# Attention into a Hyena gate on one core: rest values as 64-row couples, one PSUM pool, 1 KB query runs, halved first weights, and a new order

## The chip, the cores and the metric

One core of a Trainium2 chip runs the kernel. The metric is the device time of one execution in microseconds (us). The profile and the trace belong to one execution each and count from the first to the last instruction; that span is some 1.8 us shorter than the device time. Engines: PE is TensorE, PEld its weight loads, DVE VectorE, ACT ScalarE, POOL GpSimd, SP SyncE (it only issues transfers).

## The reference, cut to what matters

```python
# q, k, v: (8, 12, 448, 64) f32
scores = q @ k.transpose(0, 1, 3, 2) / 8
e = np.exp(scores - m)                                 # m: maximum of a row
attn = e / (e.sum(-1) + np.exp(-m) + 1e-9)             # softmax off by one
x = (attn @ v).transpose(0, 2, 1, 3).reshape(8, 448, 768)
x1, x2, x3 = np.split(x @ w_proj, 3, axis=-1)          # w_proj (768, 2304)
x2c = irfft(rfft(x2, axis=1) * rfft(filter_fft, axis=0), n=448, axis=1)
out = (x1 * x2c * x3) @ w_out                          # w_out (768, 768)
```

A sequence of 448 rows is three blocks of 128 and a rest of 64. The twelve heads are worked in six pairs, and a batch is attention for six pairs followed by the dense part (projection, filter, gate, output projection).

## The kernel before

The kernel carries its own scheduler. Every piece of work is a task with an engine, a cost in us, a wanted time, and what it needs, makes, takes and gives back. The scheduler plays the machine forward with these costs and so fixes the order of each engine's instructions. Engines then run that order strictly.

```python
class Plan:
    LANDING = 1.8            # us from the end of a transfer's share to "landed"
    def transfers(to):       # the scheduler's picture of the transfers
        ...                  # the two queues (SyncE, GpSimd) share the engines by cost
        done(h[2], clock + self.LANDING, "SP")
```

The first two batches are "staged": f32 is loaded by SyncE and cast by GpSimd or VectorE. Later batches are loaded with a cast by GpSimd (bf16 straight into one natural-layout buffer `nat` that holds `kn` and `qn`), then transposed by SyncE's DMA transposes into `kT` and `qT`.

```python
# staged query: two transfers a pair, 256 B runs
for u in range(2):
    nc.sync.dma_start(src[0:SP, 256*u : 256*u+256].rearrange("p (j d) -> p j d", j=NST),
                      q[b, 2*hp+u].rearrange("(j p) d -> p j d", j=NST))
# a later batch: its loads may start when the batch before has been transposed out of nat
room = ["zero kn" if b == NSTAGED else ("turn", b - 1)]
add("POOL", 0.95, want + STEP*n, lambda st=st: q_load(st), need=room, make=[("qn", b)], dma=1.6, ...)
... # 8 key loads, 1 value load
for u in range(2):           # the rest rows of v, copied by GpSimd to a block-diagonal tile
    nc.gpsimd.tensor_copy(vr[b % 2][c, :, u, 0:DH], vn[b % 2][c, :, 3, 0:DH])
```

Attention's output for the rest rows was one matmul over both heads, against that block-diagonal value tile:

```python
nc.tensor.matmul(op[:, n, :, :], e[0][:, o:o+128], vr[b % 2][:, hp, :, :], start=True, stop=False)
```

The dense part starts with x transposed (one transfer a pair of heads, the last pair by TensorE), then "folded" by VectorE in two groups of three pairs:

```python
add("SP", 1.3, w, x_dma, need=[("xb", i)] + old, make=[("X", i), ("xT", b, hp)], dma=0.5)
...
def first(ds, n):            # the fold
    if n == 0:
        nc.vector.tensor_copy(x[:, ds, S:S+2], x[:, ds, 0:2])
    nc.vector.tensor_tensor(t[...], lo, hi, op=(ALU.add, ALU.subtract)[n])
w = ready - (0.4 if g else PERIOD / 4)     # wanted time of the second and the first group
```

PSUM was three pools: two double banks for scores, one bank for attention's output, three for the rest.

The softmax here doesn't subtract the row's maximum and nothing guards it: scores larger than these inputs give would overflow.

Of the kernel before, what the change touches and what calls it, by code (L numbers as in the profile page):

```python
# [41 lines left out]
class Plan:  # L42
# [12 lines left out]
    OPEN = 9  # L55

    def __init__(self, rings):
        self.size = rings
        self.tasks = []

# [3 lines left out]
    def run(self):  # L64
# [9 lines left out]
        when = {}  # L74
        held = {r: [] for r in self.size}
        holds = set()
        gone = {}
        free = {e: 0.0 for e in queue}
# [6 lines left out]
        def done(t, end, by):  # L85
            for k in t[6]:
                made[k] -= 1
                when[k] = (max(end, when.get(k, (0.0, by))[0]), by)
                heapq.heappush(events, end + self.LAT[by])
                heapq.heappush(events, end)  # L90
            for tok in t[8]:
                left[tok] -= 1
                if left[tok] == 0:
                    gone[tok] = end + self.LAT[by]
                    heapq.heappush(events, gone[tok])

# [18 lines left out]

        def ready(t):
# [9 lines left out]
            if e == "SP" and t[9]:  # L126
                out = sum(h[2][12] for h in queues[e]) + sum(x > now + 1e-9 for x in landed)
                if out + t[12] > self.OPEN:
                    return False
            new = {}  # L130
            for r, tok in t[7]:
                if (r, tok) in holds:
                    continue
# [7 lines left out]
        while any(queue.values()):  # L141
            moved = False
            for e in queue:
# [8 lines left out]
                moved = True  # L152
                for r, tok in t[7]:
                    if (r, tok) not in holds:
                        holds.add((r, tok))
                        held[r].append(tok)
# [12 lines left out]
            if not moved:  # L169
                while events and events[0] <= now + 1e-9:  # L170
                    heapq.heappop(events)
                if any(queues.values()):
                    heapq.heappush(events, now + 0.1)
# [10 lines left out]
def kernel(  # L184
# [15 lines left out]
    SPIN = 40  # L200
    EARLY1 = 14.0
    SLOT1 = 5.5
    BASE2 = 77.0
    READY1 = 80.0
    READY0 = 34.0
    BPS = 8.2
    ZV = 8.0
    RE1 = 4.0
    FT = 8.0
    GATES = (  # L210
        (1, [("iv", 5), ("ir", 1), ("ik", 7), ("iq", 7)]), ("F", [("cv", 8)]), (0, [("cv", 9)]), (2, [("cv", 10)]),
        ("O", [("cv", 11)]),
    )
    STEP = 1.5
    FOLD0 = (28.5, 29.0, 29.5)
# [3 lines left out]
    psc = ctx.enter_context(tc.tile_pool(name="psc", bufs=2, space=bass.MemoryType.PSUM))  # L219
    pop = ctx.enter_context(tc.tile_pool(name="pop", bufs=1, space=bass.MemoryType.PSUM))  # L220
    phy = ctx.enter_context(tc.tile_pool(name="phy", bufs=3, space=bass.MemoryType.PSUM))
# [27 lines left out]
    vr = [const.tile([128, NHP, 2, DH + 1], BF16, name=f"vr{i}") for i in range(2)]  # L249
# [8 lines left out]
    KNAT, SLOT = NHP * 4 * 128, 1280  # L258
    nat = const.tile([128, max(KNAT + NST * D, 8 * SLOT)], BF16, name="nat")
# [4 lines left out]
    def stage(g, at, n):  # L264
        o = g % 4 * SLOT + at
# [5 lines left out]
            "sc": 2, "op": 1, "hy": 3, "e": 6, "er": 2, "k0": 2, "q0": 2, "u": 1, "w": 1, "xf": 1,  # L271
# [5 lines left out]
    ATT0, SLOT0 = 6.0, 3.5  # L277
    PERIOD = 43.5
    BASE = 31.0

    def tau(i, frac=0.0):

        if i < NHP:
            return ATT0 + SLOT0 * (i + frac)
        if i < 2 * NHP:
            return BASE + SLOT1 * (i + frac - NHP)
        return BASE2 + (i + frac - 2 * NHP) * PERIOD / NHP

# [11 lines left out]
    def staged(b):  # L300
# [3 lines left out]
        for hp in range(NHP):  # L304
# [5 lines left out]
            for n, (name, x, at, size) in enumerate(parts):  # L310
                src = stage(g, at, size)

                def load(name=name, x=x, src=src, hp=hp, g=g):
                    if name == "q":
                        for u in range(2):
                            (nc.sync if g else nc.scalar).dma_start(
                                src[0:SP, 256 * u : 256 * u + 256].rearrange("p (j d) -> p j d", j=NST),
                                q[b, 2 * hp + u].rearrange("(j p) d -> p j d", j=NST),
                            )
# [8 lines left out]
                add("ACT" if first else "SP", 1.04 if name == "q" else 0.52, -21.0 if first else want + 0.1 * n, load, need=need,  # L328
                    make=[("s" + name, g)], dma=0.97 if name == "q" else 0.64, run=256 if name == "q" else 768,
                    n=2 if name == "q" else 1, begun=[("i" + name, g)])  # L330
                if hp == 0 and name != "q":
                    add("SP", 0.5, want + (0.05 if name == "k" else SLOT0 + 0.05) if b == 0 else want - RE1 + 0.1 * n,
                        lambda name=name, x=x: nc.sync.dma_start(rests[:, "kv".index(name)], shared(x, b)),
                        need=[("cr" + name, b - 1)] if b else (), make=[("r" + name, b)],
                        dma=0.75, begun=[("ir", b)])
# [31 lines left out]
            if hp == 0:  # L367
                for u in range(2):
# [7 lines left out]
                    add("POOL", 0.56, tau(g) + 1.0,  # L376
                        lambda c=c, u=u: nc.gpsimd.tensor_copy(vr[b % 2][c, :, u, 0:DH], rests[c, 1]),
                        need=[("rv", b), ("ones", b % 2)] + ([("V", NHP * (b - 1) - 1, 1)] if b >= 2 else []), make=[("crv", b), ("vr", b)])

            def turn(g=g, hp=hp):  # L380
                T[g]["ps"] = tps = phy.tile([128, 512], F32, name="tps", tag="hy")
                tb = tps.bitcast(BF16)
                if g:
                    nc.tensor.transpose(tb[:, 0:128], ks[:, hp, :], ident_bf)
                for t in range(1, 4):
                    nc.tensor.transpose(
                        tb[:, t * 128 : (t + 1) * 128], T[g]["kn"][:, t - 1, :], ident_bf
                    )
                for j in range(NST):
# [4 lines left out]
            def k_back(g=g, hp=hp):  # L394
                tb = T[g]["ps"].bitcast(BF16)
# [8 lines left out]
            def q_back(g=g, hp=hp):  # L404
                tb = T[g]["ps"].bitcast(BF16)
                to, of = qT[b % 2][:, hp, :], tb[:, 512 : 512 + S]
# [6 lines left out]
            def turn0():  # L413
                T[0]["ps0"] = tps = phy.tile([128, 512], F32, name="tps0", tag="hy")
                nc.tensor.transpose(tps.bitcast(BF16)[:, 0:128], ks[:, 0, :], ident_bf)

            def back0():
                nc.vector.tensor_copy(kT[0][:, 0, 0, :], T[0]["ps0"].bitcast(BF16)[:, 0:128])

            if g == 0:  # L420
# [4 lines left out]
            add("PE", 0.45, w, turn, need=[("ck", g), ("cq", g), "ident"] + ([("crk", b)] if g else []), make=[("T", g)],  # L425
                take=[hy], give=[("k0", g), ("q0", g)])
            old = [("S", g - 2 * NHP, 3)] if b >= 2 else []
            back = "ACT" if g == NHP else "DVE"
            add(back, 0.33, w + 0.1, q_back, need=[("T", g)] + old, make=[("qT", g)], give=[hy])
            add(back if g else "ACT", 0.36, w + 0.2, k_back, need=[("T", g)] + old, make=[("kT", g)], give=[hy])  # L430

    def loaded(b):
# [3 lines left out]
        want = tau(i0) - 40.0  # L436
        start = want if b > NSTAGED else 0.0
        room = ["zero kn" if b == NSTAGED else ("turn", b - 1)]

        def q_load(st):  # L440
            nc.gpsimd.dma_start(
                qn[:, st].rearrange("p (h d) -> p h d", h=H),
                q[b, :, st * SP : (st + 1) * SP, :].rearrange("h p d -> p h d"),
            )

        def k_load(u, t):
            c = slice(64 * u, 64 * u + 64)
            if t < 3:
                nc.gpsimd.dma_start(kn[:, :, 1 + t, c], kr[:, :, 4 * u + t, :])  # L449
            else:  # L450
                nc.gpsimd.dma_start(kn[c, :, 0, c], kr[c, :, 3, :])

        n = 0
        for st in range(NST):
            add("POOL", 0.95, want + STEP * n, lambda st=st: q_load(st), need=room, make=[("qn", b)], dma=1.6, after=start + STEP * n)
            n += 1
        for u in range(2):
            for t in range(4):
                add("POOL", 0.85, want + STEP * n, lambda u=u, t=t: k_load(u, t), need=room,
                    make=[("kn", b)], dma=1.0, after=start + STEP * n)  # L460
                n += 1
        add("POOL", 2.05, want + STEP * n,
            lambda: nc.gpsimd.dma_start(
                vn[b % 2][:].rearrange("p g t d -> p (g t) d")[:, :, 0:DH],
                v[b].rearrange("h s d -> (h s) d").rearrange("(n p) d -> p n d", p=128),
            ),
            need=room + [("V", i0 - NHP - 1, 1)], make=[("vn", b)], dma=6.0, after=start + STEP * n)
        for u in range(2):
            c = slice(64 * u, 64 * u + 64)
            add("POOL", 0.9, want + 22.0,  # L470
                lambda u=u, c=c: nc.gpsimd.tensor_copy(vr[b % 2][c, :, u, 0:DH], vn[b % 2][c, :, 3, 0:DH]),
                need=[("vn", b), ("V", i0 - NHP - 1, 1)], make=[("vr", b)])

        def q_turn(st):
            nc.sync.dma_start(
                qT[b % 2][:, :, st * SP : (st + 1) * SP], qn[:, st], transpose=True
            )

        def k_turn(gs):
            nc.sync.dma_start(  # L480
                kT[b % 2][:, gs].rearrange("p g t c -> p (g t) c"),
                kn[:, gs].rearrange("p g t c -> p (g t c)"),
                transpose=True,
            )

        last = ("S", i0 - NHP - 1, 3)
        for st in range(NST):
            add("SP", 1.4, want + 24.0, lambda st=st: q_turn(st), need=[("qn", b), last],
                make=[("turn", b)] + [("qT", i0 + i) for i in range(NHP)], dma=0.6)
        for h in range(NHP):  # L490
            add("SP", 0.9, want + 24.0 + h, lambda h=h: k_turn(slice(h, h + 1)), need=[("kn", b), last],
                make=[("turn", b), ("kT", i0 + h)], dma=0.6)
# [68 lines left out]
    def more_tables():  # L561
        bb = lambda: W["bps"].bitcast(BF16)[:, 0 : 4 * (FQ + 1)].rearrange("p (a b) -> p a b", a=4)

        def mirror():
            W["rps"] = rps = phy.tile([128, 512], F32, name="rps", tag="hy")
# [4 lines left out]
        def mirror_back():  # L570

            rps = W["rps"]
# [619 lines left out]
```

## Time and profile before

| | before |
|---|---|
| device time, median of 3 | 388.97 us (387.98 to 389.45) |
| profiled span | 386.9 us |
| TensorE busy | 369.1 us, 95% |
| VectorE, ScalarE busy | 69%, 68% |
| TensorE idle between 60 and 370 us | 1.2 us |

The page's busy table gives time, share and number of instructions of each engine; the slices below it give busy tenths of each fortieth of the span, and PEclk the granted clock in tenths. Where a line carries `<-`, the left side is the engine, tile and line that waited and the right side what came last. The lines themselves are shown in the prediction.

Beside busy time I use a second measure throughout. Each matmul is priced by the undisturbed spacing from its start to the next one's (0.19 us for 448 columns, 0.16 for 384, 0.056 for 130, 0.03 for 65, 3 ns for the first half of a couple, and 0.093 us for each change into or out of 64-row work). **Excess** is the spacing beyond that price: idle time, a slow clock, everything. Before, the priced work is 354.0 us and the excess 25.9, of which 16.1 lies in the first 60 us, 9.2 between 60 and 370, and 0.6 behind; the rest of the span lies before the first and after the last matmul.

### The profile page before, as it was taken

What the parts mean: (1) busy time and instruction counts of PE and PEld (TensorE: products, weight loads), DVE (VectorE), ACT (ScalarE), POOL (GpSimd) and SP (SyncE); (2) the same over time, 40 slices, a digit from 0 to 9 for tenths busy, and PEclk for the clock granted to TensorE, in tenths of its full rate; (3) what the DMA queues carried; (4) which work ended last, traced back from release to release, by engine and by line L of the source; (5) the groups of instructions that cost most, each with busy time, mean ns of one, the idle gap of its engine ahead of it and who ended that gap; (6) DMA issues with size and microseconds to landing.
All of it is one profiled execution on the core that took longest, in us unless ns stands there. A gap on an engine that the chain in (4) does not pass through costs nothing.

```text
span 386.9 us, 8977 instructions
## 1 busy us (share of the span) xinstructions
PE 369.1 (95%) x3461; PEld 232.1 (60%) x3461; DVE 268.7 (69%) x817; ACT 264.3 (68%) x460; POOL 113.5 (29%) x179
## 2 busy tenths in 40 slices
PE   6767999999999999999999999999999999999995
PEld 5444766656665566556655566556755666567652
DVE  6677669872888459956698439956699439964870
ACT  5778676737876758766876768766776758743543
POOL 7765818236340713332406222332100000000000
PEclk9999999999999999999999999999999999999998
DMA  9999999999999999799989699699941321012004
GB/s 203 239 247 234 208 208 177 147 134 214 139 150 112 224 164 128 99 115 163 138 127 87 145 153 162 81 109 156 123 70 26 126 56 29 15 54 84 0 2 164
DMA packets 179419, 50.44 MB, mean 130 GB/s; under 512 B 166125, under 2 KB 175792, under 8 KB 179376
## 3 DMA queue, kind: packets, MB, share of 16 engines
q0 software_dynamic: 101680, 17.80, 64.0%
q1 hardware_dynamic: 76768, 31.83, 41.9%
q8 instruction: 27, 0.44, 0.5%
q10 hardware_dynamic: 928, 0.23, 0.3%
q14 instruction: 16, 0.13, 0.1%
HBM read 43.86 MB, written 11.01 MB: 142 GB/s over the span
## 4 chain that ended last, share of the span: by engine, by line
PE 83%; DVE 6%; DMA 5%; ACT 3%; issue 2%; POOL 1%; SPq 0%; POOLq 0%; ACTq 0%
PE pps L923 24%; PE pps L850 16%; PE ops L1035 13%; PE op L712 8%; PE sc L662 7%; DMA wproj_bf<-in_moe_w_proj_dram 3%; PE op L707 3%; PE xsp L877 3%; PE cps L962 2%; PE sc L664 2%; PE sc L923 1%; DMA nat<-in_k_dram 1%; PE spin L1113 1%; PE sc L850 1%; DVE cv L991 1%
## 5 line engine op out<-in xcount | busy, mean ns | idle before, releaser
L670 ACT ACTIVATE e<-sc 128x896 bf16<-128x896 f32 x144 | 127.5, 922 | 16.3 <-PE sc L662 15.2
L923 PE MATMUL pps<-xT,wproj_bf 128*128 128x448 bf16 x522 | 110.6, 352 | 0.1
L923 PEld LDWEIGHTS <-wproj_bf 128*128 128x128 bf16 x576 | 52.0, 97 | 45.8 <-issue 5.9
L850 PE MATMUL pps<-wproj_bf,xf 128*113 128x384 bf16 x360 | 66.7, 328 | 1.0 <-DMA wproj_bf<-in_moe_w_proj_dram 0.8
L850 PEld LDWEIGHTS <-xf 128*113 128x113 bf16 x384 | 48.6, 132 | 16.4 <-issue 5.5
L712 PE MATMUL op<-vn,e 128*128 128x65 bf16 x1152 | 56.7, 194 | 0.0
L712 PEld LDWEIGHTS <-e 128*128 128x128 bf16 x1152 | 50.3, 97 | 5.2
L1035 PE MATMUL ops<-wout_bf,yT 128*128 128x384 bf16 x270 | 49.2, 326 | 0.1
L449 POOL DMA_DIRECT2D nat<-in_k_dram x36 | 29.8, 845 | 49.1 <-DMA kT<-nat 46.1
L727 DVE TENSOR_TENSOR xb<-op,rec 128x256 bf16<-128x256 f32 x96 | 40.7, 424 | 3.3
L725 DVE TENSOR_SCALAR rec<-op 128x4 f32<-128x4 f32 x96 | 15.2, 158 | 39.6 <-PE op L712 38.5
L707 PE MATMUL op<-vr,er 128*128 128x130 bf16 x192 | 42.1, 219 | 0.5 <-DVE xb L727 0.5
L662 PE MATMUL sc<-qT,kT 64*128 64x448 bf16 x288 | 40.5, 354 | 0.8 <-DVE qT L410 0.7
L1047 ACT COPY osb<-ops 128x384 f32<-128x384 f32 x52 | 24.2, 484 | 22.9 <-PE ops L1035 22.6
L1035 PEld LDWEIGHTS <-yT 128*128 128x128 bf16 x288 | 26.5, 98 | 20.0 <-DVE yT L1006 2.5
L891 DVE TENSOR_TENSOR t<-xs,hrs 113x768 bf16<-113x768 bf16 (+1 forms) x64 | 34.2, 552 | 5.8 <-ACT xs L885 5.6
L675 ACT ACTIVATE er<-sc 128x448 bf16<-128x448 f32 x48 | 26.6, 555 | 14.6 <-PE sc L664 14.0
L862 DVE CAST x<-pps 113x384 bf16<-113x384 f32 x32 | 17.7, 555 | 25.7 <-PE pps L850 25.6
L938 DVE TENSOR_TENSOR g<-x,pps 128x448 bf16<-128x448 bf16 x45 | 27.7, 616 | 6.9 <-PE pps L923 6.6
L971 ACT CAST cr<-cps 128x452 bf16<-128x452 f32 x48 | 26.0, 549 | 9.4 <-PE cps L962 9.2
L935 ACT CAST x<-pps 128x448 bf16<-128x448 f32 x42 | 22.9, 546 | 13.6 <-PE pps L923 12.6
L885 ACT CAST xs<-xsp 113x384 bf16<-113x384 f32 (+1 forms) x60 | 26.6, 492 | 3.8 <-PE xsp L877 3.2
(117 smaller groups left out, 462.1 us busy)
## 6 DMA issues: line engine op xcount, KB each, us to landing
out_dram<-osb SPq DMA_DIRECT2D x24, 384.0 KB, 2.4
nat<-in_q_dram POOLq DMA_DIRECT2D x24, 168.0 KB, 6.6
vn<-in_v_dram POOLq DMA_DIRECT2D x6, 672.0 KB, 10.9
wproj_bf<-in_moe_w_proj_dram POOLq DMA_DIRECT2D x3, 1152.0 KB, 12.2
nat<-in_k_dram POOLq DMA_DIRECT2D x36, 96.0 KB, 3.8
nat<-in_q_dram SPq DMA_DIRECT2D x22, 112.0 KB, 5.1
nat<-in_k_dram SPq DMA_DIRECT2D x12, 192.0 KB, 4.6
nat<-in_v_dram SPq DMA_DIRECT2D x12, 192.0 KB, 4.5
```

Of the source, the lines that this page charges most:

```text
L449: nc.gpsimd.dma_start(kn[:, :, 1 + t, c], kr[:, :, 4 * u + t, :])
L662: nc.tensor.matmul(sc[:, u, 0:S], kT[b % 2][c, hp, t, :], qT[b % 2][c, hp, :])
L670: nc.scalar.activation(e[:, 0 : 2 * S].rearrange("p (u n) -> p u n", u=2), sc[:, :, 0:S], AF.Exp, scale=SCALE)
L675: nc.scalar.activation(e[:, 0:S], sc[:, 0, 0:S], AF.Exp, scale=SCALE)
L707: nc.tensor.matmul(op[:, n, :, :], e[0][:, o : o + 128], vr[b % 2][:, hp, :, :], start=True, stop=False)
L712: nc.tensor.matmul(op[:, n, u, :], e[1 + t][:, u * S + o : u * S + o + 128], vn[b % 2][:, hp, 4 * u + t, :], start=False, stop=(u == 1 and ...
L727: nc.vector.tensor_tensor(W["xb", b][:, hp, 2 * hf : 2 * hf + 2, :].rearrange("p t (u d) -> p t u d", u=2), op[:, :, :, 0:DH], rec[:].unsq ...
L850: nc.tensor.matmul(pps[:FQ, :DCH], W["xf", b][:, pg, kt, 0:FQ], wproj_bf[:, kt, D + ch * DCH : D + (ch + 1) * DCH], start=(kt == 0), stop= ...
L891: nc.vector.tensor_tensor(t[:K], L["xs", par, ch][:K], h, op=ALU.mult)
L923: nc.tensor.matmul(p[:, :S], wproj_bf[:, kt, 2 * part * D + dt * 128 : 2 * part * D + (dt + 1) * 128], xT()[:, kt, 0:S], start=(kt == 0), ...
L938: nc.vector.tensor_tensor(g[:, dt, :], L["x1", dt], p[:, :S], op=ALU.mult)
L1035: nc.tensor.matmul(ops[:n, :DCH], y[:, dt, 0:n], wout_bf[:, dt, ch * DCH : (ch + 1) * DCH], start=(dt == 0), stop=(dt == NDT - 1),)
```

## The change

The intent: give TensorE less work (rests of both heads as couples of 64-row matmuls), let any work use any free PSUM bank, move fewer and larger packets at the start, and let the first projection begin on half a weight. The order of all engines was made anew, with a wanted time for each batch where one period served all before.

```diff
 # constants of the order
-    SLOT1 = 5.5; BASE2 = 77.0; READY1 = 80.0; READY0 = 34.0; STEP = 1.5; FOLD0 = (28.5, 29.0, 29.5)
+    ATT   = [0.73, 23.91, 76.59, 113.02, 157.33, 206.03, 230.45, 288.92]
+    DENSE = [34.45, 80.23, 133.33, 185.87, 215.03, 258.15, 323.32, 386.03]
+    FOLD  = [-0.15, 9.79, 8.68, 22.52, 35.64, 2.11, 38.65, 20.48]
+    AHEAD = [0.06, 0.21, 51.70, 7.49, 23.49, 30.79, 39.19, 47.87]
+    LOADS = ((1, 0), (1, 1), ("F", None), (0, None), (2, None), ("O", None))
+    LOAD  = [29.39, 41.73, 22.32, 31.54, 44.82, 51.67]; STEP = 2.29; HALVED = (2,)
 # fold
-            w = ready - (0.4 if g else PERIOD / 4) ...
+            w = DENSE[b] - 2.5 - (0.4 if g else FOLD[b]) ...
 # PSUM: one pool of eight banks; the scheduler gives out the bank
+    psum = psp.tile([128, 8 * 512], F32, name="psum")
 # rests
-                nc.tensor.matmul(op[:, n, :, :], e[0][:, o : o + 128], vr[b % 2][:, hp, :, :], start=True, stop=False)
+            for n in range(NST):
+                for u in range(2):
+                    c = slice(64 * u, 64 * u + 64)
+                    nc.tensor.matmul(out_bank(u)[:, n, :], P["e"][0][c, n*128 : n*128+128],
+                                     vn[b % 2][c, hp, 3, :], start=(n == 0), stop=False)
 # staged queries
-                        for u in range(2): ... "(j p) d -> p j d"      # 256 B runs
+                            q[b, 2*hp : 2*hp+2].rearrange("u (p j) d -> p u (j d)", j=NST)   # 1 KB runs
 # loads of later batches
-        room = ["zero kn" if b == NSTAGED else ("turn", b - 1)]
+            def gate():
+                mark = small.tile([1, 2], BF16, name="mark")
+                nc.gpsimd.tensor_copy(mark[:, 0:1], kT[(b - 1) % 2][0:1, NHP - 1, 0, 0:1])
+                nc.gpsimd.tensor_copy(mark[:, 1:2], qT[(b - 1) % 2][0:1, NHP - 1, S - 1 : S])
+            add("POOL", 0.15, want - 0.1, gate, need=[("turn", b - 1)], make=[("gate", b)])
-        for u in range(2): nc.gpsimd.tensor_copy(vr[...], vn[...])
 ... (the rest cut: bank bookkeeping in the scheduler, renamed tiles, two passes for the third batch)
```

## The prediction

> **What bounds the kernel now.** I read the profile's busy table first, then busy time by stretches of the span, then the timeline of TensorE, then the waits and the DMA part.
>
> ```profile
> PE 369.1 (95%) x3461; PEld 232.1 (60%) x3461; DVE 268.7 (69%) x817; ACT 264.3 (68%) x460; POOL 113.5 (29%) x179
> PE   6767999999999999999999999999999999999995
> DMA  9999999999999999799989699699941321012004
> ```
>
> TensorE is the bound, and what little it idles lies at the two ends. The busy time by stretches makes that exact (columns: stretch, length, busy us of PE, PEld, DVE, ACT, POOL, granted clock, DMA share, GB/s):
>
> ```profile
> 0.01:40.00 39.99, 28.89 (x384) 20.29 (x385) 27.54 (x94) 29.80 (x43) 26.99 (x77) 1.00 1.05 232
> 40.00:60.00 20.00, 19.64 (x192) 13.25 (x190) 13.83 (x41) 14.99 (x28) 11.06 (x18) 1.00 1.12 205
> 60.00:370.00 310.00, 308.82 (x2824) 192.19 (x2823) 221.38 (x668) 214.07 (x379) 75.49 (x87) 1.00 1.11 114
> 370.00:386.86 16.86, 11.71 (x72) 6.39 (x69) 5.99 (x17) 5.48 (x12) 0.00 (x0) 0.94 0.27 95
> ```
>
> TensorE idles 11.1 us in the first 40, 0.4 in the next 20, 1.2 in the 310 us of the middle and 5.2 in the tail. The middle can only be shortened by giving TensorE less to do; the front by bringing data sooner. But a busy PE row is not one at its peak, so I also priced each matmul by the spacing from its start to the next start. From the timeline (start, length, what, xcount):
>
> ```profile
> 199.97 0.22 PE L707 MATMUL op<-vr,er 128*128 128x130 bf16 x1
> 200.03 0.35 PE L712 MATMUL op<-vn,e 128*128 128x65 bf16 x6
> 200.22 0.22 PE L707 MATMUL op<-vr,er 128*128 128x130 bf16 x1
> 200.28 0.35 PE L712 MATMUL op<-vn,e 128*128 128x65 bf16 x6
> 200.47 1.30 PE L923 MATMUL pps<-xT,wproj_bf 128*128 128x448 bf16 x6
> 201.61 0.37 PE L962 MATMUL cps<-bt,yh 113*128 113x113 bf16 x4
> 201.82 1.30 PE L923 MATMUL pps<-xT,wproj_bf 128*128 128x448 bf16 x6
> 203.05 0.55 PE L662 MATMUL sc<-qT,kT 64*128 64x448 bf16 x4
> 203.53 0.38 PE L962 MATMUL cps<-bt,yh 113*128 113x113 bf16 x4
> ```
>
> A rest matmul (L707, 130 columns) holds TensorE 0.056 us; each of the 65-column ones after it 0.031 ((200.22-200.03)/6). Six 448-column matmuls take 1.14 us (200.47 to 201.61), 0.19 each. The second six start at 201.82 and should be done at 202.96, but the scores (64 rows) start at 203.05: 0.09 us lost going in. Two couples then need 0.38, yet the next work starts at 203.53, not 203.43: 0.1 lost coming out. So **each run of 64-row matmuls costs 0.19 us** beyond its columns. The order of TensorE's instructions has 75 such runs: 14 us of the span.
>
> **What the Trainium skill says.** "TensorEngine Tiling (Array Packing)", section Tiling Modes: changing the tiling mode drains TensorE. The trace agrees, 0.09 in and 0.1 out. Its section Restrictions and Gotchas: different row tiles must not write one PSUM bank at once; this is why the changed kernel gives each head of a pair its own bank. "TensorE: Matmul & The Clock Gate", Part 3: matmuls on different row groups start about 4 ns apart; the single records show the two halves of a score couple 3 to 4 ns apart. "DMA: Bandwidth & Descriptors", Specifications: 512 B or more is needed for line rate. In the first 60 us the packet records of the hardware queue hold 12,928 packets of 256 B at a mean 21.7 ns and 6,144 of 768 B at 43.6 ns: 11.8 against 17.6 bytes per ns and engine, so the trace agrees.
>
> **The change part by part.**
>
> 1. Rest values as couples. Before, a pair of heads has 4 rest matmuls of 130 columns against a block-diagonal value tile: 4 x 0.056 = 0.22 us. Now 4 couples of 65 columns with 64 rows each, issued right behind a run of scores. If the halves of a couple overlap as scores do, a couple costs what a 65-column matmul does, 0.031: 0.125 a pair of heads. Saved 0.1 x 48 pairs = 4.8 us, all of it in the TensorE-bound stream. The built program of the changed kernel has 80 runs of 64 rows, not 75: 47 rest groups stand in score runs, one alone, and the scores are cut a little more: 5 x 0.19 = 0.95 us back. For weight loads that may not keep up with two short matmuls at a time I take off another 0.3. Net **-3.5 us**.
>
> 2. Staged queries in 1 KB runs. A line through 256 B/21.7 ns and 768 B/43.6 ns gives an estimate of 54.5 ns for 1 KB. The 12 query loads of the first two batches go from 10,752 x 21.7 ns/16 = 14.6 us of all 16 engines to 2,688 x 54.5/16 = 9.2: **5.4 us less transfer time** in a stretch in which the queues are full. Adding up that stretch before: queries 14.6, keys and values 24 x 0.70 = 16.7, rests 4 x 1.04 = 4.2, three projection weights and the output weights 4 x 6.7 = 26.7 (768 packets at 139 ns/16), filter 3.9: 66 us, and the output weights do land at 63.0. The copy back of a query now reads PSUM with a stride; some 0.1 us x 12 on DVE, which is not the bound.
>
> 3. First weights in halves, filter ahead of them. Before, the first projection starts at 36.6 us, when its 1152 KB land (issued 24.2):
>
> ```profile
> 24.16 12.41 DMA wproj_bf<-in_moe_w_proj_dram
> 36.62 1.14 PE pps L850 x6
> ```
>
> By then TensorE has done 20.6 us of priced work, so 16 us are gone (1.8 before the first matmul, some 2 to slow spin matmuls, 12 waiting for keys, queries and casts). In the changed order 23.5 us of work stand ahead of the first projection (filter spectrum and a further pair of heads among them), and it needs only a half. Ahead of that half: 9 pairs of heads at 2.16 = 19.5, rests 4.2, filter 3.9, the half 3.3, plus what shares the queues meanwhile, about 3.5: it lands near 34.5, estimated. That is 11 us lost instead of 16. But then the gates want the next third and the second half (whole transfer time up to there some 44 and 48 us) and TensorE, 8.7 us of work later, is there first by 1 or 2 us. So **-4.2 us** of the 5.4 possible.
>
> 4. One PSUM pool, third batch in halves, new priorities. Removes waits for banks. The middle has 1.2 us of idle, so **-0.5 us**. The tail (last matmul ends at 382.07; copy, store) is unchanged: 0. Two DVE memsets (0.71 each) and the copies of rest values on POOL go: beside other work, nothing.
>
> Sum -3.5 - 4.2 - 0.5 = -8.2; 388.97 - 8.2 = 380.8, and the new order has been fitted more finely than mine is read, so **380.5 us**.
>
> **The rivals.**
>
> - The couples don't overlap: eight matmuls at 0.031 = 0.25 us against 0.22. For it: start spacing of short matmuls stays near 0.03 whatever is tried in this trace. Against: score couples start 3 ns apart. Then the first part costs +2 us with the extra runs, and the time is about 386.
> - The front stays as it is: loads are hidden behind something else, such as POOL, busy 27.0 of the first 40 us with casts and DMA issues. For it: POOL still casts 12 queries at 0.63 us, and waits name its casts ahead of transposes. Against: POOL itself waits for DMAs there. Then only -4 is left: 385.
> - The front gains all that the transfers save and more: the filter and a ninth pair of heads fill the holes and the spin is 8 matmuls shorter. -6.5 there, and 377 to 378.
> - DVE or ACT becomes the bound in the middle, with 69% and 68% busy on average, because the order bunches evictions. I see no sign: idle there was 1.2 us in 310. It would cost 2 to 4 us.
>
> **Range and chances.** The first part may be -5 to -1, the front -6.5 to -1.5, the middle -1.5 to +2. Not all ends at once: 375.5 to 384.5 holds it 8 times in 10. Faster by over 2% means under 381.2, and my middle lies just under that: 0.55. Within 2% 0.43; slower 0.02.
>
> **What would show it.** Rest matmuls in pairs with starts 3 to 4 ns apart and about 0.03 us from couple to couple, 80 runs of scores, each still losing 0.19; if each of the eight takes 0.03, part 1 is wrong. Query packets of 1 KB near 55 ns; the output weights landing near 58 rather than 63 us. The first projection near 34.5 us and TensorE idle of 7 to 8 us in the first 60 instead of 11.5. Between 60 and 370 us idle of at most 1 to 2 us; more would mean that banks, evictions or late loads of a batch now hold TensorE. The prediction is wrong above all if the front waits for something that is not a transfer.

## The result

The changed kernel is slower.

| | before | changed |
|---|---|---|
| device time, same chip | 389.21 us (4 runs) | 401.45 us (400.05 to 402.9, 4 runs) |
| ratio | 1 | 1.0286, 95% interval 1.0227 to 1.0345 |
| profiled span | 386.9 | 398.2 |
| priced TensorE work | 354.0 | 349.9 |
| excess, first 60 us | 16.1 | 17.3 |
| excess, 60 us to the last 18 | 9.2 | 23.5 |

Executions over 1.5% slower than the fastest of the same kernel are left out of the means. A ratio is the mean time of one kernel's fast runs over that of the other's in the same rounds, so it is not quite the ratio of the medians. The differences add up to the 11.4 us by which the span grew: -4.1 of work (some 0.4 of it the eight spin matmuls, 32 instead of 40, that the changed kernel leaves out), +1.2 in front, +14.3 in the middle, 0 in the tail.

The page of the changed kernel, busy times and slices:

```profile
PE 370.2 (93%) x3645; PEld 234.6 (59%) x3645; DVE 266.2 (67%) x815; ACT 263.8 (66%) x460; POOL 115.3 (29%) x185
PE   5967999999999998999499998996999999999995
PEclk9897999999999999999699999999799999999999
```

Where the row of TensorE read 9 throughout the middle before, there are holes now: a slice at 4 near 190 us, with the clock at 6 in the same slice, and one at 6 near 275 us, ahead of a slice with the clock at 7. Busy time by stretches (columns as in the prediction) puts the idle of the middle at 11.7 us in 310 instead of 1.2, and the mean clock there at 0.98 instead of 1.00:

```profile
0.00:40.00 40.00, 29.48 (x383) 20.44 (x385) 26.95 (x85) 28.11 (x42) 30.18 (x79) 0.87 1.07 245
60.00:370.00 310.00, 298.28 (x2907) 187.11 (x2905) 209.10 (x645) 208.04 (x365) 75.19 (x93) 0.98 1.15 114
```

What did the largest hole wait for? The timeline of TensorE, then that of VectorE, around 190 us (start, length, what, count, then idle before and its releaser):

```profile
188.63 0.55 PE L732 MATMUL psum<-qT,kT 64*128 64x448 bf16 x4
189.02 0.19 PE L754 MATMUL psum<-vn,er 64*128 64x65 bf16 x1
194.28 0.38 PE L754 MATMUL psum<-vn,er 64*128 64x65 bf16 x7 [5.06 <-DVE x L944]
```

```profile
185.26 0.62 DVE L1020 TENSOR_TENSOR g<-x,psum 128x448 bf16<-128x448 bf16 x1
192.62 0.17 DVE L901 COPY xT<-xT 128x6 bf16<-128x6 bf16 x1 [6.74 <-DMA xT<-xb]
...
193.67 0.55 DVE L944 CAST x<-psum 113x384 bf16<-113x384 f32 x1
```

Read it backwards. TensorE stands in the middle of a group of rests from 189.2, for a PSUM bank. VectorE's L944 empties that bank, from 193.67 to 194.22. Its own data had long been there; it stands in VectorE's order behind L901, the first instruction of the fold, and the fold waits 6.74 us for a transpose of x that has not landed. The views of waits say the same of the whole span (engine, line, what for; us in total, times, longest):

```profile
POOL mark L537 <- DMA kT<-nat: 98.4, 5, 24.0
...
DVE xT L901 <- DMA xT<-xb: 15.1, 3, 6.7
...
PE psum L754 <- DVE x L944: 5.1, 1, 5.1
```

Before, no fold waited for a transfer: the first folds of batches 2 to 7 started 4.2, 0.1, 1.5, 0.8, 1.0 and 1.8 us after the last transpose that they needed had landed. In the changed kernel the first folds of batches 2 to 5 wait 0.54, 2.17, 6.74 and 2.40 us and the second of batch 5 waits 6.18: 18 us in all of VectorE. (The view of waits has 15.1 of these under the transposes; it puts those of 0.54 and 2.40 down to "issue", but they too end within 0.1 us of a landing.) And the transposes themselves land later: issue to landing took 3.7 us in the mean and 6.5 at most before, and 5.0 and 9.2 now, beside loads that come as one burst behind the marks at L537. The view of the tile, before and then changed:

```profile
DMA to landing us min/median/max: 2.4/3.4/6.5
```

```profile
DMA to landing us min/median/max: 2.4/3.8/9.2
```

The scheduler reckons 2.3 (1.8 plus its share of 0.5). Beside the longest stalls the clock is halved for a while: matmuls of 384 columns are 0.32 us apart instead of 0.16 from 196 to 199 us, and those of 448 are slowed likewise after the two stalls near 277 us. The Trainium skill's "TensorE: Matmul & The Clock Gate", Part 1, has half the clock after an idle window of about 3.4 us; this trace agrees for the stall of 5.06 us, 3.1 us into which its clock record falls to a half, and shows the same at 277.68 us, half a us into the second of two stalls of 1.5 and 1.6 us with about 1 us of work between them.

The couples, in the timeline of TensorE:

```profile
79.40 0.55 PE L732 MATMUL psum<-qT,kT 64*128 64x448 bf16 x4
79.79 0.28 PE L754 MATMUL psum<-vn,er 64*128 64x65 bf16 x8
80.01 0.93 PE L762 MATMUL psum<-vn,e 128*128 128x65 bf16 x24
```

Eight rest matmuls hold TensorE for 0.22 us with the change back to full rows (80.01 less 79.79); the single records show the two of a couple 3 to 4 ns apart and all eight starting within 96 ns. That part is as predicted. The front, from the timelines of GpSimd and of TensorE:

```profile
25.93 0.96 POOL L626 DMA_DIRECT2D filt<-in_moe_filter_fft_dram  x1 [3.15 <-ACT er L745]
...
41.98 2.12 PE L932 MATMUL psum<-wproj_bf,xf 128*113 128x384 bf16 x12
```

The filter is issued after GpSimd has stood 3.15 us, the half weight only at 32.5 us, and the first projection starts at 41.98 us, not at 34.5 (36.6 before). The packets of 1 KB took 64.3 ns in the mean, not 54.5.

### The profile page after: what moved, and what is told of

The parts are those of the page before. It is cut to its first block, busy times and chain, and to the rows that moved or that the text cites.

```text
span 398.2 us, 9460 instructions
## 1 busy us (share of the span) xinstructions
PE 370.2 (93%) x3645; PEld 234.6 (59%) x3645; DVE 266.2 (67%) x815; ACT 263.8 (66%) x460; POOL 115.3 (29%) x185
## 4 chain that ended last, share of the span: by engine, by line
PE 75%; DMA 10%; DVE 8%; issue 2%; POOL 1%; ACT 1%; SPq 1%; DVEq 0%; POOLq 0%; ACTq 0%
PE psum L1005 22%; PE psum L932 15%; PE psum L1117 12%; DMA xT<-xb 9%; PE psum L762 9%; PE psum L732 7%; PE psum L959 2%; PE psum L1044 2%; PE psum L734 2%; PE psum L754 1%; DMA nat<-in_q_dram 1%; PE psum L855 1%; DVE g L1020 1%; DVE xb L777 1%; PE psum L443 1%
## 5 line engine op out<-in xcount | busy, mean ns | idle before, releaser
L739 ACT ACTIVATE e<-psum 128x896 bf16<-128x896 f32 x144 | 125.9, 924 | 18.3 <-PE psum L732 18.3
L1005 PE MATMUL psum<-xT,wproj_bf 128*128 128x448 bf16 x576 | 123.8, 354 | 4.5 <-DVE xb L777 1.8
L932 PE MATMUL psum<-wproj_bf,xf 128*113 128x384 bf16 x384 | 73.4, 338 | 0.0
L932 PEld LDWEIGHTS <-xf 128*113 128x113 bf16 x384 | 51.2, 137 | 14.7 <-issue 1.9
L1117 PE MATMUL psum<-wout_bf,yT 128*128 128x384 bf16 x288 | 52.7, 326 | 0.4 <-DVE yT L1088 0.4
L762 PE MATMUL psum<-vn,e 128*128 128x65 bf16 x1152 | 46.5, 196 | 0.0
L777 DVE TENSOR_TENSOR xb<-psum,rec 128x256 bf16<-128x256 f32 x96 | 40.8, 424 | 3.3
L732 PE MATMUL psum<-qT,kT 64*128 64x448 bf16 x288 | 42.1, 360 | 0.7 <-DVE qT L464 0.4
L944 DVE CAST x<-psum 113x384 bf16<-113x384 f32 x32 | 17.8, 556 | 31.0 <-PE psum L932 30.8
L1129 ACT COPY osb<-psum 128x384 f32<-128x384 f32 x56 | 26.1, 484 | 18.6 <-PE psum L1117 18.4
L775 DVE TENSOR_SCALAR rec<-psum 128x4 f32<-128x4 f32 x96 | 14.9, 156 | 32.5 <-PE psum L762 32.1
L1020 DVE TENSOR_TENSOR g<-x,psum 128x448 bf16<-128x448 bf16 x48 | 29.5, 616 | 7.6 <-PE psum L1005 7.0
L745 ACT ACTIVATE er<-psum 128x448 bf16<-128x448 f32 x48 | 26.6, 555 | 9.4 <-PE psum L734 9.4
L967 ACT CAST xs<-psum 113x384 bf16<-113x384 f32 (+1 forms) x64 | 28.1, 496 | 3.7 <-PE psum L959 3.7
## 6 DMA issues: line engine op xcount, KB each, us to landing
vn<-in_v_dram POOLq DMA_DIRECT2D x5, 672.0 KB, 15.7
wproj_bf<-in_moe_w_proj_dram POOLq DMA_DIRECT2D x2, 1152.0 KB, 14.6
```

What stands on the lines that cost most here:

```text
L732: nc.tensor.matmul(sc[:, u, 0:S], kT[b % 2][c, hp, t, :], qT[b % 2][c, hp, :])
L739: nc.scalar.activation(e[:, 0 : 2 * S].rearrange("p (u n) -> p u n", u=2), pair(("sc", ("S", i, t)))[:, :, 0:S], AF.Exp, scale=SCALE,)
L745: nc.scalar.activation(e[:, 0:S], bank(("hy", ("S", i, t)))[:, 0:S], AF.Exp, scale=SCALE)
L762: nc.tensor.matmul(out_bank(u)[:, n, :], P["e"][1 + t][:, u * S + n * 128 : u * S + n * 128 + 128], vn[b % 2][:, hp, 4 * u + t, :], start= ...
L777: nc.vector.tensor_tensor(W["xb", b][:, hp, :, 64 * u : 64 * u + 64], op[:, :, 0:DH], rec[:].unsqueeze(2).to_broadcast([128, NST, DH]), op ...
L932: nc.tensor.matmul(pps[:FQ, :DCH], W["xf", b][:, pg, kt, 0:FQ], wproj_bf[:, kt, D + ch * DCH : D + (ch + 1) * DCH], start=(kt == 0), stop= ...
```

## The experiments

Twelve runs were made, on three chips; each has its own runs of the kernel before, and ratios are against those. The changed kernel itself ran again in the second call, as r_after.

> The changed kernel again, unaltered, as the reference of this call: ratio near 1.029 if the first measurement (401.45 us) stands; the results of the kernels beside it are read against this one.

Measured: 400.58 us, ratio 1.0296 (1.0254 to 1.0339). Its profiled run has an excess of 17.9 us in front and 26.0 in the middle; single stalls move by 1 to 2 us between executions, so only differences above that are read from a profile.

### Undoing the mistake in the scheduler's picture

e1_truth. The scheduler is told that a transpose of x lands 6.5 us later than it thought. Costs, constants and everything else stay; only the orders differ, and with them the PSUM banks that it hands out.

```diff
-                        done(h[2], clock + self.LANDING, "SP")
+                        done(h[2], clock + self.LANDING + h[2][14], "SP")    # h[2][14] is slow
-   add("SP", 1.3, w, x_dma, ..., make=[("X", i), ("xT", b, hp)], dma=0.5)
+   add("SP", 1.3, w, x_dma, ..., make=[("X", i), ("xT", b, hp)], dma=0.5, slow=6.5)
```

> Only the list scheduler is told that a DMA transpose of x lands 6.5 us later than it assumed (its model had about 2.3 us, the changed kernel's trace shows up to 9.2), so that whatever reads it is put later in the engines' orders. Theory A (the folds on DVE stand right behind late transposes and hold up DVE, PSUM and TensorE between 140 and 290 us): DVE's waits for xT, 18 us in all, go to under 4, the excess over the priced matmuls between 60 and 370 us falls from 23 to about 10, and the time from 401.5 to 388 to 391. Theory B (banks of the one PSUM pool or the rest couples make the stalls): 399 to 402, with TensorE still waiting for evictions.

Measured: 390.92 us, ratio 1.0005 (0.9962 to 1.0048). The wait of the fold is nearly gone:

```profile
DVE xT L901 <- DMA xT<-xb: 2.0, 2, 1.3
PE psum L1005 <- DMA xT<-xb: 1.7, 1, 1.7
```

The middle's excess is 14.7 us instead of 23.5. The transposes are as late as in the changed kernel (median 4.6 us, up to 10.2); they are merely no longer in front of other work. The largest stall left in the middle is one of 4.2 us that ends at 161 us, waiting for the transposes of the next batch's keys, which the scheduler was still told to expect after 2.4, and the clock that it costs; 1.7 us more go to TensorE's own wait for x (second line). This one number in the scheduler's picture is worth 2.8% of the time.

e2_nogate. The two marks by which GpSimd waits for the transposes of the batch before are left out; the same order otherwise.

```diff
             def gate():
-                mark = small.tile([1, 2], BF16, name="mark")
-                nc.gpsimd.tensor_copy(mark[:, 0:1], kT[...]); nc.gpsimd.tensor_copy(mark[:, 1:2], qT[...])
+                pass
```

> The two tiny GpSimd copies ahead of each later batch's loads are not emitted, everything else keeps its order. Theory A2 (the gate and the missing rest copies bunch a batch's query, key and value loads into one burst, and the burst is what slows the DMA transposes of x to 6 to 9 us): query loads start some 15 us sooner, transposes of x land in a mean of about 4 us instead of 5.0, and the time falls by 4 to 8 us, to 394 to 397. If the burst is not the reason: 400 to 402 and the same landing times.

Measured: 397.3 us, ratio 1.0172 (1.0125 to 1.022): about 1.1% less than the changed kernel by the ratios, the low end of the fall that the theory asked for. Transposes of x land after 4.6 us in the mean (5.0 in the changed kernel, about 4 expected). The stalls at 158 and 247 us are gone, those of 5.2 us that ends at 194 and of 1.6 us each near 276 are not. The bursts are part of the cause, and by far not all of it.

e5_no_later_loads. The loads of batches 3 to 7 are not issued (the result is wrong; all engines keep their order).

```diff
-   lambda st=st, gs=gs: q_load(st, None, gs)
+   lambda st=st, gs=gs: q_load(st, None, gs) if b < 3 else None      # the same for k_load and v_load
```

> The changed kernel with the loads of q, k and v for the batches after the third left out (wrong result on purpose; same order of instructions on every engine). Theory A2 (the transposes of x land late because they share the transfer engines with a burst of loads): the transposes of x in batches 3 to 7 land in a mean of about 3 us instead of 5, and the stalls of TensorE at 159, 189, 247 and 276 us, 11.6 us together with the slow clock behind them, shrink to under 3: 388 to 391 us. Rival A3 (the transposes are late for a reason of their own, such as the order on SyncE's queue or the transposes of q and k between them): landing stays near 5 us, and the time within 2 us of the changed kernel.

Measured: 383.44 us, ratio 0.9841 (0.9805 to 0.9877), lower than either theory had it. From its trace the landing of the transposes (least, median, greatest), the waits for them, and the middle by stretches:

```profile
DMA to landing us min/median/max: 2.4/2.4/4.7
```

```profile
DVE xT L901 <- DMA xT<-xb: 1.7, 2, 1.0
```

```profile
60.00:370.00 310.00, 309.70 (x3021) 194.90 (x3019) 224.47 (x685) 216.28 (x382) 16.45 (x30) 1.00 0.44 81
```

Against a landing of 2.4/3.8/9.2 in the changed kernel, a transpose of x without loads beside it takes 3.0 us in the mean. TensorE idles 0.3 us in the 310 of the middle, in the very order that lost 11.7 before. So the order isn't bad in itself; it is made for transposes that land in 2.4 us, and the loads make that untrue. The rival, that transposes are slow for a reason of their own, falls. (The run also frees GpSimd of issuing these loads, 16 us busy in the middle instead of 75, and ends all waits for the loads themselves, so the whole gain in time is not that of the transposes alone.) The Trainium skill's "DMA: Bandwidth & Descriptors", section Issuing engines are not separate DMA queues, has transfers of all issuing engines run on the same 16 engines and interleave; the trace agrees, 3.0 against 5.0 us in the mean.

### The couples

e4_rests_one_by_one. The eight rest matmuls of a pair are issued head after head, so that neighbours in program order use the same rows.

```diff
-            for n in range(NST):
-                for u in range(2):
+            for u in range(2):
+                for n in range(NST):
```

> The eight rest matmuls of a pair of heads in the order of the heads, four of one and then four of the other, so that no two neighbours are of different row groups. If the couples overlap as the prediction said: each group takes 8 x 0.03 = 0.24 us instead of 0.125, so TensorE's priced work rises by 5.5 us and the time to 405 to 407. If the couples never overlapped: unchanged, 400 to 402.

Measured: 399.87 us, ratio 1.0233 (1.0187 to 1.028), and 112 ns from the first to the last start of a group instead of 96. Both theories missed: the order of issue costs 16 ns a group, not 115. In the program the wait for the second head's bank stands on its fifth matmul; in the trace the record that carries this wait starts second in 27 of 48 groups. So TensorE seems to start a matmul of the other row group ahead of three earlier ones. The experiment therefore doesn't price overlap; the group itself does: 96 ns from the first start to the last and 0.03 us for the last make 0.13 us, against the 0.22 us of four wide matmuls before.

### The front

e3_filter_buffer. The filter is loaded into the space of the output weights, so that no buffer has to come free.

```diff
-        W["F"] = F = hyp.tile([FQ, 4, D], BF16, name="filt", tag="yT")
+        W["F"] = F = wout_bf[0:FQ, 0:4, :]
```

> The filter is loaded into the still unused output weights' buffer instead of the buffer of the sine table, same order otherwise. Theory C (the front gained nothing because GpSimd's queue stood 3.1 us before the filter load for that buffer, and the casts and weight loads behind it came late): the filter load is issued near 22.8 instead of 25.9 us, TensorE's 2.1 and 1.1 us stalls near 30 us and the throttled clock behind them go, the first projection starts at 38 to 39 instead of 42.0, time down by 3 to 4 us to 397.5 to 398.5. Rival (the front waits for transfers only): the first projection stays within 1 us of 42 and the time at 400 to 402.

Measured: 398.41 us, ratio 1.0206 (1.0155 to 1.0256); the first projection at 41.80. GpSimd stands just as long, now with nothing to wait for:

```profile
POOL wout_bf L626 <- issue: 3.1, 1, 3.1
```

So it was no buffer. The time fell inside theory C's range although none of its signs came: luck. The difference of 0.8% lies where the intervals still touch, and no wait of the profile accounts for it.

e6_first_dma_early. One transfer of two elements is issued by GpSimd at 17.6 us, ahead of the filter.

```diff
             nc.gpsimd.memset(vn[i][:, :, :, DH : DH + 1], 1.0)
+            if i == 1:
+                nc.gpsimd.dma_start(wout_bf[0:1, 0, 0:2], moe_w_out[0:1, 0:2])
```

> The changed kernel with one tiny transfer issued by GpSimd (two elements) at about 16.5 us, where GpSimd waits for TensorE anyway. Theory C2 (the first transfer that GpSimd issues makes it stand some 3 us, whatever it is): the idle of 3.15 us before the filter load at 22.8 us goes and appears behind 16.4 us instead, the filter is issued near 23 to 24 us, TensorE's stalls of 2.07 and 1.07 us at 29 and 30 us shrink, and the time falls by 1 to 4 us. Rival C3 (it is this place in the program, for instance the fetching of instructions): the idle stays at 22.8, and the time within 1 us.

Measured: 398.09 us, ratio 1.0188 (1.0145 to 1.0231). The timeline of GpSimd:

```profile
17.61 0.78 POOL L1220 DMA_DIRECT2D wout_bf<-in_moe_w_out_dram  x1
...
23.51 0.76 POOL L626 DMA_DIRECT2D filt<-in_moe_filter_fft_dram  x1
```

The 3.15 us are gone from the filter, as the theory of a first transfer says. (e9 below agrees: there the half weight is GpSimd's first transfer, 3.26 us stand ahead of it and none ahead of the filter.) They do not appear at the tiny one, where the theory looked for them; behind that one GpSimd stands 1.7 us for a staged key anyway, which may hide them. TensorE's stalls at 29 and 30 us, for GpSimd's casts, shrink from 3.1 to 0.35 us together. Yet the first projection starts at 42.27, and the excess of the front is 17.6 us against 17.3 and 17.9: the filter lands at 34.19 although it was issued 2.4 us sooner (34.27 in the changed kernel), and TensorE's wait for its sums, ahead of the filter's spectrum, grows from 1.5 to 2.5 us. The time fell by 1.1% against r_after all the same (by the ratios); the profiled run does not show where.

e8_queries_in_256B. The second part of the change undone: 256 B runs and a straight copy back; the same order.

```diff
-   q[b, 2*hp : 2*hp+2].rearrange("u (p j) d -> p u (j d)", j=NST)       # one transfer
+   for u in range(2): ... q[b, 2*hp+u].rearrange("(j p) d -> p j d", j=NST)
-   to, of = qT[...].rearrange("p (n j) -> p n j", j=NST), tb[...].rearrange("p (j n) -> p n j", j=NST)
+   to, of = qT[...], tb[:, 512 : 512 + S]
```

> The changed kernel with its second part undone: staged queries again in 256 B runs, two transfers a pair of heads and the straight copy back, everything else in the same order. Theory D (what is transferred up to the first projection's weight sets the front): with the packet times measured (21.5 ns for 256 B, 64.3 ns for 1 KB) the queries cost 14.4 instead of 10.8 us of all engines, so the first projection starts 2 to 4 us later than the 41.98 us of the changed kernel, and the time grows by 2 to 4 us against it: 403 to 405 us. Rival D2 (the transfers of the front are hidden, GpSimd's casts and issues set it): the first projection within 1 us, and the time within 1 us of 400.6.

Measured: 405.36 us, ratio 1.0359 (1.0306 to 1.0411), an interval that overlaps those of the changed kernel (1.0286 and 1.0296), so a loss against it is not shown beyond the noise. The time is about what the transfer theory asked for, but its sign is missing: the first projection starts at 40.80, earlier than with 1 KB runs, and the front's excess is 16.4. What is longer stands in the middle, above all in a stall of 3.5 us that ends at 126 us, for the transposes of keys. Later weights and the output weights land some 3 us later (74.9 against 70.2 to 71.8). A number that came near for a wrong reason: nothing here shows that the 1 KB runs shorten the front.

e9_half_weight_before_filter. The wanted times of filter and first half weight are exchanged.

```diff
-    LOAD = [29.39, 41.73, 22.32, 31.54, 44.82, 51.67]
+    LOAD = [22.32, 41.73, 29.39, 31.54, 44.82, 51.67]
```

> The changed kernel with the first half weight issued ahead of the filter instead of behind it. Theory D (transfers in order of issue): the half weight lands where the filter landed, near 34 us instead of 40.9, and the filter some 3 us later than now; the first projection starts near 35 to 37 us, and if nothing in the middle gets worse the time falls by 2 to 4 us. Rival: the filter's spectrum is wanted first anyway by the gates, so TensorE waits as long for it and the time stays within 1 us; the middle's stalls may also move by 2 us either way because the order differs.

Measured: 403.44 us, ratio 1.0316 (1.0268 to 1.0364). The half weight lands at 32.8 and the filter at 39.1, about as expected, and the first projection starts at 42.03 all the same; theory D had 35 to 37. The last group of the first batch's fold, which it also needs, starts at 39.6, behind TensorE's own attention work; in the changed kernel that group starts at 41.1, right beside the landing of the half weight at 40.9. So the weight was not alone in holding the projection. The front's excess is 18.4.

### A version from the cause

e7_truth_nogate_first. The late landing of x (6.5 us) and of q and k (5 us), no marks, and the tiny early transfer.

> Everything together: the scheduler told that a transpose of x lands 6.5 us later and one of q or k 5 us later than it assumed, no marks that gate the loads, and the tiny early transfer. Theory A: the middle's excess falls to that of the kernel before (about 9 us) and the front gains 2 to 3: 383 to 388 us. Rival (each repair only shifts the wait to the next buffer): 390 us or more, as with the first repair alone.

Measured: 389.59 us, ratio 1.0005 (0.9961 to 1.0049); expected 383 to 388. The front gains (excess 15.2), the folds no longer stall TensorE, and a new wait has come at 132 us:

```profile
ACT osb L1127 <- DMA out_dram<-osb: 6.9, 1, 6.9
...
PE psum L752 <- ACT osb L1127: 4.9, 1, 4.9
```

Output tiles are stored by the same queue, and beside the loads the three stores issued from 123 to 126 us took 8.6 to 9.2 us too, which nobody had told the scheduler. Repairing some kinds of transfer moved the wait to the next: the rival's mechanism was right, its number (390 or more) missed by 0.4.

e10_reordered_a and e11_reordered_b. So every transfer of SyncE that ends within 3 us of a GpSimd load is now reckoned to land 6 us later, whatever it carries:

```diff
+                if "POOL" in heads:
+                    cast = clock
-                        done(h[2], clock + self.LANDING, "SP")
+                        late = self.LANDING + (6.0 if e == "SP" and clock - cast < 3.0 else 0.0)
+                        done(h[2], clock + late, "SP")
```

The constants of the order were searched again under this picture, by the end that the scheduler itself reckons for 4, 6 and 8 us, two searches of some thousand trials each; the tiny early transfer is in, the rest of the changed kernel untouched.

> The changed kernel whose order has been made anew for a scheduler that reckons a transfer of SyncE to land 6 us later while loads of GpSimd are on their way (the mechanism that the run without later loads showed), with the tiny early transfer. Theory A: stalls of the middle between 60 and 370 us fall from 23 us to under 11 (the kernel before has 8.6), the couples' 4 us stay, and the time is 381 to 387 us, under that of the kernel before. Rival (landing times scatter too much for any fixed order): 388 us or more, stalls of 3 us and more at new places.

> As the run before, with another order found for the same assumption. Theory A: 381 to 387 us. Rival: 388 us or more; if the two orders differ by over 1 per cent, the scatter of single waits and not the mechanism decides the last few us.

Measured: 385.84 us, ratio 0.9885 (0.9831 to 0.9938), and 385.51 us, ratio 0.9883 (0.9849 to 0.9916). Both are correct and beat both kernels: 1.2% under the kernel before (both intervals stay below 1), 3.9% under the changed one by the ratios. Of the second, the landing of the transposes and the middle by stretches:

```profile
DMA to landing us min/median/max: 2.4/4.3/9.8
```

```profile
60.00:370.00 310.00, 306.91 (x2988) 192.61 (x2988) 223.08 (x679) 214.96 (x381) 75.57 (x92) 1.00 1.26 114
```

The transposes land as late as in the changed kernel, and no fold waits for one: the first folds of batches 2 to 7 now follow their last transpose by 9.5, 9.3, 3.5, 8.4, 14.1 and 3.1 us. The middle's excess is 9.5 us (6.3 in the first of the two), back at that of the kernel before. The transfers were not made faster; the order stopped depending on them. These two kernels change many constants at once, and no search of the same length was made under the old picture, so that the new picture alone gave the 1.2% is not shown; the proof of the mechanism remains the pair of e1 and e5.

| kernel | ratio to before | excess in front | excess in the middle |
|---|---|---|---|
| changed (first, again) | 1.0286, 1.0296 | 17.3, 17.9 | 23.5, 26.0 |
| x lands late (e1) | 1.0005 | 17.2 | 14.7 |
| no marks (e2) | 1.0172 | 18.1 | 19.3 |
| no later loads (e5) | 0.9841 | 18.2 | 5.8 |
| combined (e7) | 1.0005 | 15.2 | 14.8 |
| reordered (e10, e11) | 0.9885, 0.9883 | 20.5, 16.0 | 6.3, 9.5 |

The front is the first 60 us, the middle runs from there to about 18 us before the end; both are from the one profiled execution.

## Why the prediction was wrong

The step that failed above all is the fourth, and with it the dismissal of the last rival: of the 19.6 us between the predicted sum of -8.2 and the measured +11.4, it makes up 14.8. The third, the front, makes up 5.4; the first was better than predicted by 0.6.

- **Rest couples: right.** Predicted -3.5 us of net work; the priced work fell by 4.1, the spin's 0.4 among them. Pairs start 3 to 4 ns apart, a group takes 0.13 us as reckoned, and there are 80 runs of 64 rows, each still costing 0.19. That a group ends with TensorE going back to full rows was already in the term for the runs.
- **1 KB queries: right in kind, too large in size.** 64.3 ns a packet, not 54.5, so 2,688 of them take 10.8 us of all engines against the 14.6 before: 3.8 us less instead of 5.4. The line through two sizes was no good guide: the 768 B packets slowed too, from 43.6 to 47.7 ns. The bound of 512 B in the Trainium skill's "DMA: Bandwidth & Descriptors", Specifications, which the prediction cited, agrees with r_after: in its first 60 us packets of 256 B, 768 B and 1 KB took 21.1, 48.2 and 65.3 ns, that is 12.1, 15.9 and 15.7 bytes per ns and engine, so above the bound 1 KB gave no more than 768 B. But the transfers of the queries do not set the front (e8), so the term had no business in the sum for it.
- **Front, -4.2 us: wrong.** It came out at +1.2. I counted bytes ahead of the half weight and took its issue for granted; it was issued at 32.5 and landed at 40.9, and the first projection needed a fold that came no sooner. The output weights, which I had landing near 58, were issued at 60.7 and landed at 70.2. The rival named in the prediction, that the front stays as it is because of GpSimd's casts and issues, is nearer. But e3, e6, e8 and e9 each removed or moved one wait there, and the front's excess stayed between 16.4 and 18.4 each time: casts, transfers and TensorE's own order stand at nearly the same height. What a real gain there needs stays open; e7 has 15.2 us, which is within the scatter of one profile of what the kernel before has.
- **Middle, -0.5 us: wrong, and three quarters of the error.** It came out at +14.3. The prediction took the 1.2 us of idle before as all that the middle could change by, and the finer order as a gain ("the new order has been fitted more finely than mine is read"). It said of a bunched order on VectorE "I see no sign". The sign was in the trace: the transposes of x took up to 6.5 us, the scheduler's own constant says 2.3, and the folds followed them by as little as 0.1 us. The diff alone is no such sign: where one figure of 10.9 us set how far the first fold is wanted ahead of the dense part, there is now one for each batch, from 2.11 to 38.65 in batches 1 to 7, but the fold of the batch with 38.65 starts 9.9 us after its last transpose and that of the batch with 35.64 waits longest. A finer fit to a wrong constant is closer to the edge, not safer. It was VectorE that stood, as the rival said, but standing in line for a transfer, not busy; and the clock made the longest stalls dearer.
- **The range.** 375.5 to 384.5 was built from sizes of gains with at most +2 for the middle, and no term for an order that meets late data; a slower kernel got a chance of 0.02. (The third rival's 377 to 378 is 378.5 by its own terms.) It should have had such a term, because the change replaced the order of every engine.

Three things stay open: what the 3.15 us of GpSimd ahead of its first transfer are made of, where e6 and e3 gained their 1%, and what the one PSUM pool is worth, which no run took out by itself.

## What to carry to other kernels

Where a static order is made from assumed costs, check each assumed latency against the trace under load, and look at the slack that the order leaves behind each transfer; on an engine that runs in order, as VectorE here, one instruction placed ahead of late data stops everything behind it, even on other engines. A change that improves such an order by its own reckoning should be read with suspicion if it moves consumers closer to transfers. And repair the picture for all transfers that share the engines at once: told about one kind only, the order merely moves its wait to the next.

## What the Trainium skill lacked or had wrong

- "DMA: Bandwidth & Descriptors", Issuing engines are not separate DMA queues: that transfers interleave is said, but not what it does to a small one. A DMA transpose of one pair of heads took 2.4 us to land at least and up to 9.2 (the changed kernel) and 10.6 us (e10) beside cast loads of GpSimd; output stores went from 2.3 to 9.2 us (e7).
- "TensorE: Matmul & The Clock Gate", Part 3, has matmuls start and end strictly in program order. In e4 the record with the second head's wait starts second, not fifth, in 27 of 48 groups; this is read from where a wait stands in the records, not from a test made for it.
- The same page, Part 1, has the clock fall after an idle window of about 3.4 us, and does not say how much work within one keeps it up. At 277.68 us of the changed kernel it fell after 3.4 us in which TensorE had idled only 2.0, in two pieces.
- No page that I read has the 3.1 us for which GpSimd stands ahead of the first transfer that it issues (e3), and which is gone there when a tiny transfer goes first (e6) and stands ahead of the half weight when that goes first (3.26 us, e9).
